# Linear attention and a folded feed-forward: the first loads on GpSimd's queue, and another order of the work

## The chip, the core and the metric

The kernel runs on one core of one Trainium2 chip. The metric is device time in microseconds for one execution, input and output in the chip's main memory (HBM). A core has five engines that run their own instruction streams and meet at semaphores: PE (TensorE, the matrix unit), DVE (VectorE), ACT (ScalarE), POOL (GpSimd) and SP (SyncE, which here only starts transfers). Transfers are started from a queue of SP, GpSimd or ACT and carried out by 16 DMA engines.

## What is computed

q, k and v are float32 of shape (8 batches, 8 heads, 576 positions, 64). Linear attention with the feature map phi(x) = elu(x) + 1 gives 4608 tokens of width 512, and a multiplicative feed-forward with two more matrices follows:

```python
q_p, k_p = (phi(q), phi(k))                       # phi(x) = where(x > 0, x, exp(x) - 1) + 1
kv = np.einsum('bhsd,bhse->bhde', k_p, v)
z = np.sum(k_p, axis=2)
num = np.einsum('bhsd,bhde->bhse', q_p, kv)
den = np.einsum('bhsd,bhd->bhs', q_p, z)[..., None] + 1e-06
x = (num / den).transpose(0, 2, 1, 3).reshape(4608, 512)
a = x @ w1          # 512 x 1024
b = x @ w2          # 512 x 1024
h = a * b @ w3      # 1024 x 1024
out = h @ w_out     # 1024 x 512
```

## The kernel before

**The fold.** Nothing nonlinear stands between w3 and w_out, so the kernel makes one matrix, wf = w3 w_out, once, and then computes out = (a * b) wf. For each of the eight blocks of 128 rows of w3, step `w` (w3_tr, L450) transposes the block on PE in eight 128x128 pieces and copies it to SBUF, and step `W` (wf_mm, L459) multiplies it with w_out in eight matmuls of 512 columns; `U` is a first half of a `W`.

**Tiles and chunks.** The 576 positions of a batch are four interleaved tiles of 128 ("J" tiles) and a remainder of 64. The remainders of two batches share a tile. The 36 tiles of 128 tokens make nine chunks of four: chunk 0 is batch 0's J tiles, chunk 1 batch 1's, chunk 2 begins with the shared remainder of batches 0 and 1 and goes on with batch 2, and so on.

**Steps.** All work is cut into small steps, and a text, ORDER, lists them by hand. Each engine executes its instructions in that order and can't pass one that waits. A name is a letter, a batch or chunk, and a part; a "+" is an alternative form of the step. The letters:

- L, M, N: load k, q, v of a batch (load_qkv, L105). Part 0 and 1 are four heads each (512 KB), 2 is all eight (1 MB), 3 is the remainder, two transfers of 64 KB.
- E, C, B: load a block of w3, half of w_out, a quarter of the columns of both w1 and w2 (two transfers). These come from GpSimd's queue[...]. I: constants (I0 the identity for transposes, on GpSimd; I2 the zeros for H). H n: n matmuls on zeros, which keep PE busy.
- x, X: exp of k, q on ACT; y, Y: minimum with 1 on DVE; z, Z: the larger of it and x + 1 on DVE. Together they are phi.
- v: v to bf16. K: k^T v and z, on PE. T: transposed q by DMA (SP's queue only). A: numerator, denominator and quotient. P, D: transposed x for the feed-forward, by PE or by DMA.
- a, b, c, d, e, f, g, r: the same for batch 0, by a way without the round trip of x through a transpose (q transposed on PE, quotient by Ln and Exp on ACT, result written straight to xt).
- F c.f: for chunk c, 128 of the 1024 columns of a and b: 8 matmuls of 512 columns, a copy on ACT and a product on DVE. h and i are F0.0 and F0.1 cut by row blocks of w1 and w2, so that they can follow batch 0's attention piece by piece.
- O c.m: 128 tokens of output, 8 matmuls; S: its store, on SP's queue. Q: the last one.

An O of any chunk needs the whole fold. An F of chunk c needs xt of its four tiles and a quarter of w1 and w2 for each two f.

**What decides when a transfer starts.** SP and GpSimd start transfers in the order of their own lists and wait in line: for a buffer (k, q, v and the w3 blocks share a pool of five 1 MB buffers, L56; the remainders have eight small ones), and, since the transfers of a queue use eight completion semaphores in turn, for the eighth transfer before. GATES (L502) adds a few waits of a load for an earlier load. In load_qkv only part 3 can go to GpSimd (with "+", L111); the big parts go to SP (L120):

```python
return nc.sync.dma_start(
    out=t[:, h0 * W:h1 * W].rearrange("p (h x) -> p h x", x=W),
    in_=src[b, h0:h1, 0:NJ * P, :].rearrange("h (p j) d -> p h (j d)", j=NJ))
```

The order of the front in before: GpSimd starts three w3 blocks and all of w_out first, while SP starts k's remainder, q and k of batch 0 by halves, then v; transposes and matmuls of the fold (w0, w1, U0, W0, ...) stand among the first steps of batch 0's attention; w1 and w2 come after, F0.0 and F0.1 last, and F0.2 to F0.7 among the first steps of batch 1's attention.

Of the kernel before, what the change touches and what calls it, by code (L numbers as in the profile page):

```python
# [18 lines left out]
def kernel(  # L19
# [11 lines left out]
    nc = tc.nc  # L31
# [73 lines left out]
    def load_qkv(name, src, b, part, alt=False):  # L105


        if part == 3:
            t = raw[name + "r", b] = ldr.tile([P, RW], F32, tag="ldr", name=f"{name}32r")
            for hh in range(2):  # L110
                (nc.gpsimd if alt else nc.sync).dma_start(  # L111
                    out=t[hh * R:(hh + 1) * R].rearrange("p (h d) -> p h d", d=D),
                    in_=src[b, hh * 4:(hh + 1) * 4, NJ * P:S, :].rearrange("h p d -> p h d"))
            return None
        if (name, b) not in raw:
            raw[name, b] = ld.tile([P, JW], F32, tag="ld", name=f"{name}32")
        t = raw[name, b]
        h0, h1 = ((0, 4), (4, 8), (0, 8))[part]
        W = NJ * D
        return nc.sync.dma_start(  # L120
            out=t[:, h0 * W:h1 * W].rearrange("p (h x) -> p h x", x=W),
            in_=src[b, h0:h1, 0:NJ * P, :].rearrange("h (p j) d -> p h (j d)", j=NJ))

# [344 lines left out]


    ORDER = """  # L470
    L0.3 E0 I0 M0.0 x0.2 N0.3 E1 X0.0 w0 y0.2 M1.3 E2 w1 L0.0 x0.0 Y0.0 M0.1 N0.0 X1.2 X0.1 C0
    w2 Z0.0 C1 U0 Z0.1 W0 L0.1 y0.0 N1.3 z0.4 N0.1 a0.0 I1 Y0.1 Z0.2 Z0.3 E3 z0.0 U1 I2 U2 v0.0+
    b0.0 x0.1 w3 v0.2 W1+ a0.1 W2 v0.1+ H9 z0.1 L1.2 E4 y0.1 b0.1 c0.0 z0.2 E5 L1.3+ U3 d0.0
    e0.0 z0.3 E6 w4+ M1.2 E7 f0.0 B0 x1.0 W3+ c0.1 w5 g0.0 U4 d0.1 y1.0 x1.2 z1.0 W4+ x1.1 e0.1
    f0.1 w6+ e0.2 v1.2+ g0.1 Y1.2 f0.2 W5 M2.3+ w7 N1.0 g0.2 B1 y1.2 y1.1 z1.1 B2 W6 z1.2 W7+
    N1.1 M0.3 e0.3 X1.0 Y1.0 h0.0 f0.3 N2.3 B3 z1.3 h0.1 M2.2 Z1.0 Z1.1 v1.0 L2.3+ z1.4 X1.1
    h0.2 g0.3 K1.0+ Y1.1 Z1.2 h0.3 Z1.4 v1.1 a1.0 L2.2 i0.0 K1.1+ b1.0 Z1.3 i0.1 F0.2 a1.1 b1.1
    X2.2 T1.1 F0.3 A1.0 F0.4 F0.5 Y2.2 X0.2 A1.1 P1.1 X2.0 P1.0+ Y2.0 F0.6 Z2.4 Z2.0 X2.1 F0.7
    P1.2 x2.0 O0.1 Y2.1 Y0.2 Z2.1 P1.3+ L3.3 Z2.2 O0.0 y2.0 Z2.3 N3.3+ z2.0 x2.2 z2.1 v2.2 N2.2
    O0.2+ x2.1 Z0.4 a2.0 b2.0+ y2.1 A1.2 z2.2 M3.2 y2.2 F1.0 L3.2 z2.4 F1.1 x3.2 v2.1 z2.3 a2.1  # L480
    v2.0 b2.1+ F1.2 F1.3 K2.0+ T0.1 K2.1+ y3.2 F1.4 X3.0 A2.0 x3.0 M4.2 F1.5 z3.4 X3.1 y3.0 r0
    z3.0 D1.1 Y3.0 F1.6 L4.3 N3.2 M4.3 O0.3 Y3.1 A2.1 F1.7 z3.1 S0.0 N4.3 S0.1 Z3.0 M3.3+ M6.3
    X3.2 S0.2 X4.2 X4.0 Z3.1 Z3.2 X4.1 Y3.2 Z3.3 O1.2 D2.0 Z3.4 O1.3+ a3.0 x4.2 O1.0+ Y4.1 y4.2
    v3.2+ N4.2 L4.2 a3.1 N6.3 v3.0+ x3.1 v3.1+ y3.1 b3.0 O1.1 b3.1 F2.0 z3.2 z3.3 T2.1 T3.1 Y4.0
    F2.1 N5.3+ z4.4 K3.0+ S0.3 Z4.0 Y4.2 F2.2 K3.1+ Z4.1 Z4.2 F2.3 Z4.3 Z4.4 A3.0 x4.0 v4.0 L5.2
    L5.3 F2.4 F2.5 A3.1 y4.0 F2.6 z4.0 z4.1 x4.1 P3.1 F2.7 A2.2 P3.2 v4.1+ P3.0 O2.2 M5.2 M5.3
    x5.0 y4.1 T4.0 P3.3+ X5.2 A3.2 x5.2 S1.2 z4.2 F3.0 X5.0 z4.3 v4.2+ y5.2 X5.1 F3.1 y5.0 F3.2
    S2.2 K4.0+ x5.1 Y5.0 K4.1+ Z5.0 y5.1 z5.0 O2.3 N5.2 Z5.1 S1.0 Y5.2 A4.0 F3.3 S1.3 v5.0+ F3.4
    A4.1 D3.1 Z5.4 D2.1 L6.3 O2.0 Y5.1 v5.2 L6.2 F3.5 Z5.2 Z5.3 F3.6 v5.1+ O2.1 X6.2 F3.7 T4.1
    S1.1 z5.1 x6.0 Y6.2 O3.3 y6.0 D4.0 z5.2 z5.3 T5.0 z5.4 O3.1+ T5.1 F4.0 A4.2 x6.2 M6.2 K5.0+  # L490
    F4.1 F4.2 K5.1+ Z6.4 X6.0 F4.3 S2.3 X6.1 A5.0 F4.4 z6.0 L7.2 Y6.0 F4.5 M7.3 N6.2 S3.1 y6.2
    L7.3 F4.6 A5.1 z6.1 Z6.0 D4.1 Z6.1 Y6.1 x6.1 N7.3 S2.1 F4.7 x7.0 x7.1 S3.3 z6.4 A5.2 S2.0
    O3.2 y6.1 O4.0+ D5.0 O4.3 X7.2 Z6.2 z6.2 S3.2 v6.2 x7.2 Z6.3 y7.1 O4.2 M7.2 S4.0 O3.0 v6.0
    F5.0 T6.0 y7.0 z6.3 v6.1 F5.1 K6.0+ Y7.2 F5.2 F5.3 K6.1+ O4.1 S3.0 X7.0 z7.0 Z7.4 X7.1 T6.1
    A6.0 y7.2 F5.4 A6.1 Y7.1 F5.5 F5.6 z7.1 F5.7 D5.1 T7.1 Y7.0 N7.2 z7.4 A6.2 S4.2 Z7.0 S4.3
    v7.1 z7.2 D6.0 Z7.1 v7.2 z7.3 O5.1 Z7.2 v7.0 O5.2+ Z7.3 D6.1 O5.0 S4.1 S5.2 F6.0 S5.1 T7.0
    F6.1 F6.2 K7.0+ K7.1+ F6.3 F6.4 A7.0 F6.5 F6.6 S5.0 A7.1 F6.7 O6.2 O5.3+ O6.0+ A7.2 O6.3+
    D7.0 F7.0 F7.1 O6.1 D7.1 F7.2 F7.3 F7.4 F7.5 F7.6 S6.0 S6.2 F7.7 F8.0 O7.3 F8.1 S5.3 F8.2
    O7.0+ S7.3 F8.3 S6.1 S6.3 O7.2 F8.4 F8.5 F8.6 F8.7 O8.3+ O8.0 O8.1 S7.0 S8.3 S8.0 O7.1 S8.1
    S7.2 S7.1 Q8.2  # L500
    """
    GATES = "E4<M0.1 L0.0<E0 L1.2<E3 M0.0<E0 M1.2<C1 N1.0<E7"  # L502
    ctx.enter_context(tc.manual_schedule())
    src = {"k": k, "q": q, "v": v}
    held = {}
    gates = dict(g.split("<") for g in GATES.split())
    OBUF = 5
# [9 lines left out]
    def step(s):  # L517
# [25 lines left out]
        elif t in "LMN":  # L543
            name = "kqv"["LMN".index(t)]
            ins = load_qkv(name, src[name], b, i, alt)
            loaded(s, ins)
        elif t == "B":
# [83 lines left out]
```

## Time and profile before

| | us |
|---|---|
| median of 8 runs | 261.21 |
| lowest, highest | 260.42, 262.31 |
| the profiled execution | 261.07 |
| its span on the core | 259.0 |

The profile is one execution. Its span runs from the core's first instruction to its last; 2.07 us of the execution lie around it. Engine times are busy times; a busy PE is one with a matmul under way. The 16 DMA engines moved 48.98 MB in the span, of which the queue of GpSimd ("software_dynamic", q0) carried 6.03 MB and that of SP ("hardware_dynamic", q1) 42.54 MB; bytes are counted as written, so a weight that is turned into bf16 counts half of what is read. 38.80 MB were read from HBM: 28.3 of q, k, v and 10.5 of weights. Median times from issue to landing:

| transfer | queue | count | size written | us to landing |
|---|---|---|---|---|
| k, whole | SP | 7 | 1024 KB | 8.4 |
| q, whole | SP | 7 | 1024 KB | 8.6 |
| q, half | SP | 2 | 512 KB | 10.3 |
| w3 block | GpSimd | 8 | 256 KB | 7.4 |
| quarter of w1 or w2 | GpSimd | 8 | 256 KB | 11.4 |
| half of w_out | GpSimd | 2 | 512 KB | 11.1 |

### The profile page before, as it was taken

The numbers are of one execution on the slowest core, as the hardware profiler recorded it, in microseconds if no ns is written. First come the engines' busy times: TensorE is split into PE (matmuls) and PEld (weight loads), VectorE is DVE, ScalarE is ACT, GpSimd is POOL, SyncE is SP. The second block draws the span as 40 slices with busy tenths as digits, with TensorE's granted clock in tenths as the row PEclk, the third lists the DMA queues.
The fourth block names the chain that finished last, engine by engine and source line by source line (L and its number), as shares of the span: only waits on it lengthen the run. The fifth ranks groups of instructions, "written<-read, shape, count | busy, mean of one in ns | idle before, by whom it ended". The sixth has DMA issues, their size and how long they took to land.

```text
span 259.0 us, 4507 instructions
## 1 busy us (share of the span) xinstructions
PE 237.0 (91%) x1656; PEld 115.8 (45%) x1673; DVE 167.9 (65%) x426; ACT 129.1 (50%) x205; POOL 21.1 (8%) x42
## 2 busy tenths in 40 slices
PE   1138999899999999999999999999999999999994
PEld 1124454445454454454444444454445444444442
DVE  0026787869988979997978589468866643424320
ACT  2048587868468664677354545736533203331321
POOL 8001655000101000000000000000000000000000
PEclk9999999999999999999999999999999999999999
DMA  6999999999898499939988985844980134003024
GB/s 96 212 261 377 303 233 237 214 344 295 294 268 271 69 343 216 316 94 258 214 178 236 375 176 122 229 117 124 224 219 27 27 64 124 0 29 133 3 82 162
DMA packets 70085, 48.98 MB, mean 189 GB/s; under 512 B 34416, under 2 KB 64368, under 8 KB 70064
## 3 DMA queue, kind: packets, MB, share of 16 engines
q1 hardware_dynamic: 63104, 42.54, 61.3%
q0 software_dynamic: 6816, 6.03, 14.1%
q8 instruction: 13, 0.21, 0.3%
q10 hardware_dynamic: 144, 0.13, 0.1%
q14 instruction: 8, 0.07, 0.1%
HBM read 38.80 MB, written 9.44 MB: 186 GB/s over the span
## 4 chain that ended last, share of the span: by engine, by line
PE 76%; DMA 17%; ACT 2%; SPq 1%; issue 1%; POOL 1%; DVE 0%; POOLq 0%
PE a_ps L371 24%; PE b_ps L371 23%; PE o_ps L390 21%; DMA w3b<-in_moe_w_dram 5%; DMA k<-in_k_dram 4%; DMA v<-in_v_dram 4%; PE kvp L199 3%; DMA xt<-xn 3%; PE nd L265 2%; SPq L111 1%; PE tp L309 1%; PE xtp L285 1%; PE o_ps L417 1%; POOL k32r L111 1%; POOL w3b L445 0%
## 5 line engine op out<-in xcount | busy, mean ns | idle before, releaser
L371 PEld LDWEIGHTS <-w_sb 128*128 128x128 bf16 x576 | 54.2, 98 | 63.6 <-issue 0.7
L377 DVE TENSOR_TENSOR ab<-a_sb,b_ps 128x512 bf16<-128x512 f32 x72 | 49.0, 684 | 47.3 <-PE b_ps L371 35.7
L371 PE MATMUL a_ps<-xt,w_sb 128*128 128x512 bf16 x288 | 75.1, 380 | 0.3 <-DMA xt<-xn 0.2
L371 PE MATMUL b_ps<-xt,w_sb 128*128 128x512 bf16 x288 | 74.9, 379 | 0.0
L376 ACT COPY a_sb<-a_ps 128x512 f32<-128x512 f32 x72 | 41.9, 585 | 57.0 <-PE a_ps L371 55.8
L390 PE MATMUL o_ps<-wf_sb,ab 128*128 128x512 bf16 x266 | 63.2, 379 | 0.7
L390 PEld LDWEIGHTS <-ab 128*128 128x128 bf16 x280 | 26.7, 98 | 30.8
L393 ACT COPY o_sb<-o_ps 128x512 f32<-128x512 f32 x24 | 14.0, 583 | 30.7 <-PE o_ps L390 30.7
L162 DVE SCALAR_TENSOR_TENSOR kj<-k,e 128x256 bf16<-128x256 f32 x64 | 23.6, 414 | 0.1
L162 DVE SCALAR_TENSOR_TENSOR qj<-q,e 128x256 bf16<-128x256 f32 x64 | 23.4, 415 | 0.1
L141 DVE TENSOR_SCALAR e<-e 128x1024 bf16<-128x1024 bf16 x32 | 13.4, 418 | 13.9 <-ACT e L137 13.9
L137 ACT ACTIVATE e<-q 128x1024 bf16<-128x1024 f32 x16 | 16.7, 1058 | 9.3 <-DMA q<-in_q_dram 9.2
L454 PE MATMUL w3p<-ident,w3b 128*128 128x128 bf16 x64 | 6.2, 254 | 15.4 <-ACT w3t L455 8.0
L137 ACT ACTIVATE e<-k 128x1024 bf16<-128x1024 f32 x16 | 16.9, 1056 | 3.8 <-DMA k<-in_k_dram 2.3
L275 DVE TENSOR_TENSOR xn<-nd,r 128x512 bf16<-128x512 f32 x28 | 18.0, 685 | 0.0
L464 PE MATMUL wf_ps<-wo_sb,w3t 128*128 128x512 bf16 x61 | 16.3, 406 | 1.3 <-ACT w3t L455 1.2
L454 PEld LDWEIGHTS <-w3b 128*128 128x128 bf16 x64 | 4.8, 114 | 17.2 <-DMA w3b<-in_moe_w_dram 9.1
L393 DVE COPY o_sb<-o_ps 128x512 f32<-128x512 f32 x11 | 7.6, 686 | 6.5 <-PE o_ps L390 6.4
L171 ACT CAST vt<-v 128x1024 bf16<-128x1024 f32 x9 | 9.3, 1047 | 2.6 <-DMA v<-in_v_dram 2.6
L464 PEld LDWEIGHTS <-w3t 128*128 128x128 bf16 x64 | 6.2, 105 | 8.1 <-ACT w3t L455 1.7
L199 PE MATMUL kvp<-vt,kj 64*128 64x130 bf16 x224 | 9.2, 217 | 0.5 <-ACT vt L171 0.5
L203 ACT COPY kvf<-kvp 128x260 f32<-128x260 f32 x14 | 5.2, 375 | 8.9 <-PE kvp L199 8.7
(81 smaller groups left out, 162.7 us busy)
## 6 DMA issues: line engine op xcount, KB each, us to landing
out_dram<-o_sb SPq DMA_DIRECT2D x31, 256.0 KB, 3.2
k<-in_k_dram SPq DMA_DIRECT2D x7, 1024.0 KB, 8.4
q<-in_q_dram SPq DMA_DIRECT2D x7, 1024.0 KB, 8.6
v<-in_v_dram SPq DMA_DIRECT2D x6, 1024.0 KB, 7.5
w3b<-in_moe_w_dram POOLq DMA_DIRECT2D x8, 256.0 KB, 7.4
v<-in_v_dram SPq DMA_DIRECT2D x4, 512.0 KB, 8.7
w_sb<-in_moe_w_dram POOLq DMA_DIRECT2D x8, 256.0 KB, 11.4
out_dram<-o_sb SPq DMA_DIRECT2D x9, 128.0 KB, 2.4
```

Of the source, the lines that this page charges most:

```text
L137: nc.scalar.activation(out=e, in_=x, func=AF.Exp)
L141: nc.vector.tensor_scalar_min(out=e, in0=e, scalar1=1.0)
L162: nc.vector.scalar_tensor_tensor(out=out, in0=x, scalar=1.0, in1=e, op0=ALU.add, op1=ALU.max)
L199: nc.tensor.matmul(kvp[:, r, i * W:(i + 1) * W], kk[rows], vv[rows], start=(n == 0), stop=(n == (NJ if r == g else NJ - 1)))
L275: nc.vector.tensor_tensor(out=dst.rearrange("p (c u) e -> p u c e", u=2), in0=v4[:, :, :, 0:D], in1=r[0:n].unsqueeze(3).to_broadcast([n, 2 ...
L371: nc.tensor.matmul(ps, w[:, kc, f * P:(f + 1) * P], xt[:, 4 * c:4 * c + 4, kc, :], start=(kc == 0), stop=(kc == KC - 1))
L376: nc.scalar.copy(out=a_sb, in_=a_ps)
L377: nc.vector.tensor_mul(out=abs_[c][:, f, :], in0=a_sb, in1=b_ps)
L390: nc.tensor.matmul(o_ps, ab[:, f, m * P:(m + 1) * P], wf_sb[:, f, :], start=(f == 0), stop=(f == FC - 1))
L393: copy_of(alt)(out=o_sb, in_=o_ps)
L454: nc.tensor.transpose(tp[:, kc, :], raw["w3", i][:, kc * P:(kc + 1) * P], ident)
L464: nc.tensor.matmul(wfs[i], w3ts[i][:, kc, :], wo_sb[:, kc, :], start=(kc == 0), stop=(kc == FC - 1))
```

## The change

Three things are changed together.

1. A big part of q, k or v can now be loaded from GpSimd's queue as well, where its step has a "+".
2. With that, all k, q, v of batches 0 and 1 (except batch 0's k remainder, which stays on SP) are loaded by GpSimd, in one line with the weights: q and k of batch 0 by halves, v of batch 0, then k1, B0, E1, C0, B1, C1, B2, E2, E3, q1, B3, E4 to E7 with v1 between. Of the later batches several loads move to GpSimd too; SP keeps 9 of its 28 big loads.
3. The order is another one throughout. At the front, batch 0's attention (a to g) stands ahead of nearly all of the fold, F0.2 to F0.7 among the fold's steps, and the fold ends (W7) among the quotients of batch 1 (A1.0, A1.1); H12 stands in place of H9, before the first step of PE. Of the transposes of q for batches 2 and 3, PE's (a, b) go and DMA's (T) come; of x's, batch 2's are now done by PE (P).

No other function is changed, and no arithmetic. The diff, with ORDER cut to its front, to the first steps of chunk 1:

```diff
@@ -117,7 +117,7 @@
         t = raw[name, b]
         h0, h1 = ((0, 4), (4, 8), (0, 8))[part]
         W = NJ * D
-        return nc.sync.dma_start(
+        return (nc.gpsimd if alt else nc.sync).dma_start(
             out=t[:, h0 * W:h1 * W].rearrange("p (h x) -> p h x", x=W),
             in_=src[b, h0:h1, 0:NJ * P, :].rearrange("h (p j) d -> p h (j d)", j=NJ))
 
@@ -468,38 +468,38 @@
     ORDER = """
-    L0.3 E0 I0 M0.0 x0.2 N0.3 E1 X0.0 w0 y0.2 M1.3 E2 w1 L0.0 x0.0 Y0.0 M0.1 N0.0 X1.2 X0.1 C0
-    w2 Z0.0 C1 U0 Z0.1 W0 L0.1 y0.0 N1.3 z0.4 N0.1 a0.0 I1 Y0.1 Z0.2 Z0.3 E3 z0.0 U1 I2 U2 v0.0+
-    b0.0 x0.1 w3 v0.2 W1+ a0.1 W2 v0.1+ H9 z0.1 L1.2 E4 y0.1 b0.1 c0.0 z0.2 E5 L1.3+ U3 d0.0
-    e0.0 z0.3 E6 w4+ M1.2 E7 f0.0 B0 x1.0 W3+ c0.1 w5 g0.0 U4 d0.1 y1.0 x1.2 z1.0 W4+ x1.1 e0.1
-    f0.1 w6+ e0.2 v1.2+ g0.1 Y1.2 f0.2 W5 M2.3+ w7 N1.0 g0.2 B1 y1.2 y1.1 z1.1 B2 W6 z1.2 W7+
-    N1.1 M0.3 e0.3 X1.0 Y1.0 h0.0 f0.3 N2.3 B3 z1.3 h0.1 M2.2 Z1.0 Z1.1 v1.0 L2.3+ z1.4 X1.1
-    h0.2 g0.3 K1.0+ Y1.1 Z1.2 h0.3 Z1.4 v1.1 a1.0 L2.2 i0.0 K1.1+ b1.0 Z1.3 i0.1 F0.2 a1.1 b1.1
-    X2.2 T1.1 F0.3 A1.0 F0.4 F0.5 Y2.2 X0.2 A1.1 P1.1 X2.0 P1.0+ Y2.0 F0.6 Z2.4 Z2.0 X2.1 F0.7
-    P1.2 x2.0 O0.1 Y2.1 Y0.2 Z2.1 P1.3+ L3.3 Z2.2 O0.0 y2.0 Z2.3 N3.3+ z2.0 x2.2 z2.1 v2.2 N2.2
-    O0.2+ x2.1 Z0.4 a2.0 b2.0+ y2.1 A1.2 z2.2 M3.2 y2.2 F1.0 L3.2 z2.4 F1.1 x3.2 v2.1 z2.3 a2.1
...
+    L0.3 M0.0+ X0.0 L0.0+ I1 Y0.0 x0.2 y0.2 M0.1+ Z0.0 x0.0 Z0.1 y0.0 I2 z0.0 z0.4 L0.1+ N0.3+
+    x0.1 H12 N0.0+ N0.1+ X0.1 L1.3+ E0 Y0.1 v0.0 L1.2+ v0.1 z0.1 y0.1 B0 v0.2+ I0 Z0.2 z0.2 Z0.3
+    E1 C0 x1.2 a0.0 B1 b0.0 C1 c0.0 M1.3+ z0.3 d0.0 e0.0 a0.1 e0.1 f0.0 f0.1 B2 E2 c0.1 y1.2 E3
+    b0.1+ M1.2+ w0 d0.1 g0.0 e0.2 e0.3 f0.2 g0.1 B3 h0.0 f0.3 E4 x1.0 g0.2 z1.4 h0.1 h0.2 g0.3
+    h0.3 i0.0 y1.0 i0.1 x1.1 w1 z1.0 F0.2 X1.2 z1.1 N1.3+ y1.1 F0.3 U0 z1.2 W0+ F0.4 E5 M2.3+
+    F0.5 Y1.2 X1.0 w2+ E6 Y1.0 Z1.0 N1.0+ w3 W1 W2+ X1.1 F0.6 U3 Z1.1 E7 N1.1+ Y1.1 w4 M2.2+
+    Z1.2 W3 v1.0+ a1.0 Z1.3 b1.0 w5 F0.7 X2.2 Y2.2 Z1.4 z1.3 w6 W4 w7 L2.2+ a1.1 v1.1+ b1.1 W5+
+    v1.2 K1.0+ L3.3+ K1.1+ L2.3+ W6 X2.0 X2.1 A1.0 Y2.0 Z2.0 x2.0 W7 N2.3+ x2.1 x2.2 A1.1 T1.1
+    P1.1 O0.0 O0.1 Y2.1 Z2.4 N2.2+ P1.0 L3.2+ y2.2 y2.0 Z2.1 M0.3+ O0.3 z2.0 y2.1 v2.1 P1.2 Z2.2
+    P1.3+ v2.0 z2.1 z2.2 X0.2 Z2.3 Y0.2 z2.4 v2.2+ A1.2 x3.0 T2.0 z2.3 O0.2 M3.3+ S0.3 F1.0 x3.2
...
     """
-    GATES = "E4<M0.1 L0.0<E0 L1.2<E3 M0.0<E0 M1.2<C1 N1.0<E7"
+    GATES = "B0<L0.1 C0<N0.1 E4<N0.1 M1.2<C1"
     ctx.enter_context(tc.manual_schedule())
```

More of the change, by code (lines that the diff above doesn't have):

```diff
@@ L477 @@
-    h0.2 g0.3 K1.0+ Y1.1 Z1.2 h0.3 Z1.4 v1.1 a1.0 L2.2 i0.0 K1.1+ b1.0 Z1.3 i0.1 F0.2 a1.1 b1.1
-    X2.2 T1.1 F0.3 A1.0 F0.4 F0.5 Y2.2 X0.2 A1.1 P1.1 X2.0 P1.0+ Y2.0 F0.6 Z2.4 Z2.0 X2.1 F0.7
-    P1.2 x2.0 O0.1 Y2.1 Y0.2 Z2.1 P1.3+ L3.3 Z2.2 O0.0 y2.0 Z2.3 N3.3+ z2.0 x2.2 z2.1 v2.2 N2.2
-    O0.2+ x2.1 Z0.4 a2.0 b2.0+ y2.1 A1.2 z2.2 M3.2 y2.2 F1.0 L3.2 z2.4 F1.1 x3.2 v2.1 z2.3 a2.1
-    v2.0 b2.1+ F1.2 F1.3 K2.0+ T0.1 K2.1+ y3.2 F1.4 X3.0 A2.0 x3.0 M4.2 F1.5 z3.4 X3.1 y3.0 r0
-    z3.0 D1.1 Y3.0 F1.6 L4.3 N3.2 M4.3 O0.3 Y3.1 A2.1 F1.7 z3.1 S0.0 N4.3 S0.1 Z3.0 M3.3+ M6.3
@@ L483 @@
[L483 to L500, printed above, removed]
+    L0.3 M0.0+ X0.0 L0.0+ I1 Y0.0 x0.2 y0.2 M0.1+ Z0.0 x0.0 Z0.1 y0.0 I2 z0.0 z0.4 L0.1+ N0.3+
@@ new lines @@
+    v1.2 K1.0+ L3.3+ K1.1+ L2.3+ W6 X2.0 X2.1 A1.0 Y2.0 Z2.0 x2.0 W7 N2.3+ x2.1 x2.2 A1.1 T1.1
+    P1.1 O0.0 O0.1 Y2.1 Z2.4 N2.2+ P1.0 L3.2+ y2.2 y2.0 Z2.1 M0.3+ O0.3 z2.0 y2.1 v2.1 P1.2 Z2.2
+    P1.3+ v2.0 z2.1 z2.2 X0.2 Z2.3 Y0.2 z2.4 v2.2+ A1.2 x3.0 T2.0 z2.3 O0.2 M3.3+ S0.3 F1.0 x3.2
+    M3.2+ F1.1 X3.0 Y3.0 K2.0+ y3.0 K2.1+ N3.3 X3.1 F1.2 S0.1 M4.3 F1.3 Z0.4 z3.0 x3.1 y3.2 N3.2
+    z3.4 X3.2 F1.4 A2.0 Y3.1 F1.5 M4.2+ T0.1 F1.6 A2.1 P2.1 L4.3 v3.2+ F1.7 Z3.0 Y3.2 D1.1 Z3.1
+    S0.0 Z3.2 O1.0 y3.1 P2.2+ X4.2 L4.2 z3.1 r0 Z3.3 v3.1 O1.1+ N4.3 v3.0+ P2.0 X4.0 z3.2 O1.3
@@ new lines @@
+    F2.0 T2.1 N5.3 z3.3 T3.0 N4.2+ Z3.4 K3.0+ X4.1 A2.2 Y4.0 Y4.2 F2.1 P2.3 K3.1+ Z4.0 x4.0 y4.0
+    F2.2 M5.3 Y4.1 O1.2 z4.0 Z4.4 A3.0 F2.3 L6.3 Z4.1 L5.3 x4.2 Z4.2 F2.4 M5.2 x4.1 P3.0+ S0.2
+    T3.1 P3.1 z4.1 Z4.3 F2.5 F2.6 A3.1 X5.0 F2.7 v4.2+ v4.0 y4.1 X5.2 L5.2 P3.2 z4.2 X5.1 S1.0
+    O2.2+ S1.1 A3.2 y4.2 P3.3+ T4.0 Y5.0 v4.1 z4.3 x5.0 O2.3+ z4.4 F3.0 F3.1 x5.1 K4.0+ K4.1+
+    y5.0 Y5.2 z5.0 Z5.4 S1.3 Z5.0 M6.3 x5.2 T4.1 F3.2 F3.3 Z5.1 D3.1 z5.1 O2.1 Y5.1 A4.0 S1.2
+    x6.2 L7.3 Z5.2 F3.4 N5.2 F3.5 S2.3 D2.1 L6.2 v5.1 y5.1 A4.1 z5.2 M6.2+ F3.6 D4.0 y6.2 F3.7
@@ new lines @@
+    X6.0 S2.2 z5.3 v5.0+ O2.0 S2.1 O3.0 Z5.3 x6.0 x6.1 O3.2 M7.3 y5.2 T5.0 L7.2 z5.4 Y6.0 O3.3
+    v5.2+ y6.0 F4.0 X6.1 X6.2 K5.0+ Y6.2 K5.1+ F4.1 Y6.1 F4.2 z6.0 F4.3 M7.2 Z6.0 N6.2 A5.0 Z6.4
+    F4.4 Z6.1 F4.5 A5.1 Z6.2 O3.1 N6.3 F4.6 T5.1 z6.4 F4.7 y6.1 v6.1 S2.0 D5.0 S3.0 v6.2 z6.1
+    z6.2 X7.0 O4.0+ Z6.3 Y7.0 x7.0 y7.0 O4.1+ S3.2 x7.2 T6.0 v6.0 O4.3 A4.2 z6.3 K6.0+ D4.1 F5.0
+    F5.1 A5.2 X7.1 K6.1+ F5.2 N7.2+ A6.0 T6.1 S3.3 Z7.0 F5.3 X7.2 F5.4 S3.1 D5.1 Y7.1 F5.5 A6.1
+    Z7.1 O4.2+ N7.3 y7.2 v7.0 S4.1 A6.2 F5.6 x7.1 F5.7 Z7.2 y7.1 Z7.3 O5.0+ z7.4 Y7.2 S4.0 D6.0
@@ L501 @@
+    S4.3 Z7.4 z7.0 S5.0 O5.1 v7.1 z7.1 O5.2+ F6.0 v7.2 z7.2 T7.1 O5.3 z7.3 K7.0+ K7.1+ F6.1 F6.2
+    F6.3 T7.0 S4.2 S5.3 A7.0 F6.4 F6.5 A7.1 F6.6 F6.7 S5.1 D7.0 O6.2+ A7.2 O6.3+ O6.0 F7.0 F7.1
+    S6.3 D7.1 S5.2 S6.0 F7.2 F7.3 F7.4 O6.1 F7.5 F7.6 F7.7 D6.1 F8.0 F8.1 S6.1 O7.1 S6.2 F8.2
+    F8.3 F8.4 F8.5 O7.3 F8.6 F8.7 S7.3 O7.0+ O8.0+ S7.1 O7.2+ S7.0 O8.1 O8.3 S7.2 S8.1 S8.0 S8.3
+    Q8.2
     """
-    GATES = "E4<M0.1 L0.0<E0 L1.2<E3 M0.0<E0 M1.2<C1 N1.0<E7"
+    GATES = "B0<L0.1 C0<N0.1 E4<N0.1 M1.2<C1"
```

## The prediction

> **What bounds the kernel now.** I read the busy table and the slices first, then busy time by stretches, then the chain of waits, then the DMA queues in two short stretches.
>
> The page's first two parts: engine, busy time and share; then tenths in 40 slices of 6.5 us.
>
> ```profile
> PE 237.0 (91%) x1656; PEld 115.8 (45%) x1673; DVE 167.9 (65%) x426; ACT 129.1 (50%) x205; POOL 21.1 (8%) x42
> ...
> PE   1138999899999999999999999999999999999994
> ```
>
> TensorE is the bound, except in the first four slices and the last. By stretches (us, then busy time and instructions of PE, PEld, DVE, ACT, POOL, then clock, DMA share, GB/s written):
>
> ```profile
> 0.00:17.00 17.00, 2.11 (x17) 1.69 (x18) 1.15 (x4) 3.75 (x5) 5.35 (x18) 1.00 0.97 167
> 17.00:26.00 9.00, 7.77 (x49) 4.23 (x50) 5.08 (x15) 6.71 (x9) 1.00 (x2) 1.00 1.11 369
> 26.00:44.00 18.00, 17.41 (x118) 9.10 (x118) 13.39 (x33) 12.49 (x18) 11.69 (x18) 1.00 1.22 257
> 44.00:63.00 19.00, 18.29 (x162) 9.52 (x161) 16.04 (x43) 14.20 (x23) 0.62 (x1) 1.00 1.22 273
> 63.00:180.00 117.00, 116.53 (x898) 56.50 (x906) 97.25 (x265) 68.19 (x112) 2.45 (x4) 1.00 0.83 219
> 180.00:255.40 75.40, 74.86 (x421) 34.79 (x424) 34.93 (x72) 23.43 (x41) 0.00 (x0) 1.00 0.35 93
> ```
>
> After 63 us PE is idle for about 1 us in 192. Nearly all lost time lies in the first 26 us, while DMA is full. A gain must come from the front. The chain of waits (start, us, what) agrees:
>
> ```profile
> 1.25 3.82 DMA w3b<-in_moe_w_dram
> ...
> 8.58 11.51 DMA k<-in_k_dram
> ...
> 27.45 9.43 DMA w3b<-in_moe_w_dram
> ...
> 38.48 10.06 DMA v<-in_v_dram
> ```
>
> The last front wait is v of batch 1, landed at 48.5. PE's timeline:
>
> ```profile
> 17.77 3.24 PE L464 MATMUL wf_ps<-wo_sb,w3t 128*128 128x512 bf16 x8
> ...
> 26.99 2.10 PE L100 MATMUL warm<-zero 128*128 128x512 bf16 x9
> ...
> 37.82 1.89 PE L464 MATMUL wf_ps<-wo_sb,w3t 128*128 128x512 bf16 x8
> ...
> 61.66 1.03 PE L371 MATMUL b_ps<-xt,w_sb 128*128 128x512 bf16 x4
> ```
>
> Eight equal matmuls take 3.24 us early and 1.89 later: with the last one's 0.38 taken off, 0.41 and 0.216 us each. The last row is the end of F0.7, 62.7 us. There before has done all of the fold, chunk 0's F units, and of batch 1 its K, A1.0, A1.1, P1.0 and P1.1. I measure the change to that same state. Last, the queues (packets, MB written, share of 16 engines), at 20 to 23 and at 35 to 38 us:
>
> ```profile
> q1 hardware_dynamic: 1244, 1.14, 109.3%
> ```
>
> ```profile
> q0 software_dynamic: 778, 0.53, 116.7%
> q1 hardware_dynamic: 97, 0.09, 11.5%
> ```
>
> SP's queue alone moves 1.14 MB in 3 us, 0.38 MB/us. GpSimd's queue, with little beside it, writes 0.53 MB of bf16, so reads up to 1.06 of float32: with the other queue 1.15 in 3 us, 0.38; if some of it was uncast remainder rows, about 0.35.
>
> [...]
>
> **The change, part by part.**
> *Loads.* No byte is added. Before, SP's and GpSimd's queues shared the DMA engines, so the first q half took 9.8 us; after, one queue brings things in the listed order. Sizes follow from the shapes (a q, k or v is 1.05 MB and 0.13 of rest; B 1.05 read, C 1.05, E 0.52). Cumulated MB: batch 0's k, q, v 3.4; B0 6.2; C0 7.7; B1 8.8; C1 9.8; B2 11.0; E3 12.1; M1.2 13.1; B3 14.15; E5 15.3; E7 17.0; N1.1 17.6. From 3 to 48.5 us the queues wrote 5.0 MB (software) and 6.8 (hardware); with the cast part doubled about 16.4 MB read, 0.36 MB/us. I take 0.37, between this and 0.38. The first w3b landed 3.8 us after issue at 1.25, of which 0.52 MB is 1.4: so landing = 3.65 + MB/0.37. Batch 0 complete 12.9, B0 20.4, B1 27.4, C1 30.1, B2 33.4, E3 36.4, M1.2 39.1, B3 41.9, E7 49.6, N1.1 51.1.
> *GpSimd's issue.* Each DMA waits for the eighth before it; 2 to 3 MB (5 to 8 us of transfer) stay in flight, so the queue shouldn't run dry. A half takes the 0.75 us of an equally fine w_sb; 1 MB I put at 1.0 to 1.5 us (no row). To N1.1 that is some 32 us of issue in 50: hidden. Buffer waits (q1 on q0's buffer, the second w3 tile on k0's) are for work done 10 us earlier. Ident stands behind B0's issue, about 13 us; only the first transposes of q need it.
> *Batch 0's attention.* k is in ACT's hands by 10, v's second half is cast at about 14. DVE has 5 minima (0.42) and 16 products (0.415) plus small ones, finishing at about 16.6; then kvz/kvn 0.8, and four Ln/Exp pairs of 1.32 in row with one w3t copy of 1.0: about 24.5; product and last h matmuls: 26.4. F0.2 can start at 26.4 and B1 lands at 27.4: the attention is hidden by one us, a thin cover; where it goes, each us late costs nearly a us.
> *H12 for H9.* H9 held PE for 2.1 us at 27, amid work. H12 lies at 9 to 14, where PE has nothing: no cost. PE idles mostly from 14 to 22 afterwards, so it may be cold again at 27[...]; I take 0.5.
> *PE from 27.6.* An F unit 1.73, W 1.73, U 0.86, w 0.45, q_tr 0.45. F0.2, F0.3 to 31.1; U0, W0 32.8; wait for B2 33.4; F0.4, F0.5 36.9; w2, w3 37.8; W1 39.5; W2 needs the w2 copy, which stands on ACT behind q1's exp (M1.2 39.1 + 1.06 + 1.0 = 41.2): to 42.9; F0.6 44.6; U3, w4, W3, q_tr, w5 47.7; F0.7 49.4; w6, W4, w7, q_tr 52.5; W5 54.2; K1.0 and K1.1 (v cast by about 52.5) 55.6; W6, A1.0, W7, A1.1, two P 60.0. Against 62.7: 2.7 us earlier.
> *Later.* Transposes of q of batches 2 and 3 leave PE (32 of 0.056, 1.8 us) and go to SP's DMA (4.8 us each, with F units to cover them); 16 xt transposes come (0.9): 0.9 us less. F, O, K, A and tail count the same. SP no longer carries the early loads, so its transposes and stores wait less.
> *Sum.* -2.7 - 0.9 + 0.5 = -3.1; I keep 0.3 back for new gaps of PE after 60 us, since before has almost none there: -2.8. The profiled execution is 261.07 (span 259.0 and 2.07 outside), so 258.3; its time is 0.14 under the median of 261.21, within their spread of 1.9.
>
> **Rivals.**
> *One queue is slower (the other side).* From 3 to 6.5 us GpSimd's queue had 95% of the engines and the two read only about 0.29 MB/us; float32 1 KB rows in 1 MB requests on it are never seen. The state above then ends 8.5 us after E7 (w7, q_tr, W5, K, W6, W7 and the small ones). Break-even is 63.6 (62.7 plus the 0.9), so E7 at 55.1, a rate of 0.33 MB/us. At 0.32 the end is 263; at 0.30, 266.5. Against it: 35 to 38 us.
> *The front's gain is given back.* DVE is busy 97 of 117 us from 63 to 180; if batch 2's phi or transposes are then late for F2, the 3 us reappear as PE gaps there: 261, no change. For it: that load. Against: batch 2's q and k land right behind N1.1, by 57, earlier than now.
> *The stream runs at 0.385 and PE stays warm.* Then only PE's own work and the w2 copy bind, the state comes at 58.6: 256.
>
> **How the numbers follow.** 0.3%, what measurement can tell here, is 0.8 us. Forecast and the faster variant 0.54 (own range 255 to 260.3), given back 0.13, slower 0.33. The range 254.8 to 263.5 takes the case of one queue down to about 0.315 MB/us and leaves out about 0.2. Faster 0.54, same 0.13, slower 0.33.
>
> **What would show it.** Right: q0 carrying the front at 0.37 MB/us of reads without gaps, v of batch 1 landed at 50 to 52, F0.2 starting at 27 to 28, PE full from there, the fold's last matmul at about 59. Wrong: GpSimd's issues much over 1.5 us, DMA share below 0.9 between 5 and 50 us, F0.0 finished after 30, or PE gaps at F1.0, F2.0.

## The result, and the profile after

| | us |
|---|---|
| before, 32 runs, median (lowest, highest) | 261.26 (260.33, 262.47) |
| changed, 11 runs, median (lowest, highest) | 258.0 (256.52, 259.93) |
| ratio, 95% interval | 0.9875 (0.9853 to 0.9897) |

The changed kernel is 3.3 us faster; the forecast was 258.3. Four executions far above the others of their kernel (263.74 us of the changed one, 262.99 and 264.32 in run 4, 266.1 in run 7) are left out of all medians and ratios, and since the first of them was the one profiled with this result, the lines below are of another execution of the changed kernel: 258.04 us, span 256.2.

The page's busy row for TensorE and its row of the slices:

```profile
PE 235.5 (92%) x1641; PEld 114.0 (45%) x1660; DVE 167.1 (65%) x425; ACT 130.5 (51%) x206; POOL 42.8 (17%) x69
...
PE   0478989999999999899999999999999999999994
```

The same stretches as before (us, then busy time and instructions of PE, PEld, DVE, ACT, POOL, then clock, DMA share, GB/s):

```profile
0.00:17.00 17.00, 5.97 (x30) 2.70 (x30) 8.16 (x24) 8.99 (x10) 14.62 (x30) 1.00 0.85 285
17.00:26.00 9.00, 7.68 (x53) 4.09 (x55) 5.39 (x13) 7.56 (x12) 4.17 (x7) 1.00 1.32 197
26.00:44.00 18.00, 16.10 (x89) 7.26 (x88) 10.11 (x22) 8.70 (x13) 7.87 (x12) 1.00 1.22 237
44.00:63.00 19.00, 18.33 (x181) 10.37 (x183) 13.51 (x38) 14.60 (x22) 11.20 (x16) 1.00 0.99 280
...
63.00:180.00 117.00, 115.26 (x894) 55.83 (x901) 97.24 (x266) 68.98 (x114) 4.97 (x6) 1.00 0.92 230
```

In the first 17 us, DVE is busy for 8.16 us where it was 1.15, and ACT for 8.99 where it was 3.75: batch 0's phi is nearly done by then. PE's busy time there is mostly H12, which computes nothing of the output. Between 63 and 180 us, PE now idles 1.74 us where it idled 0.47. PE's timeline shows the places:

```profile
27.47 1.04 PE L371 MATMUL b_ps<-xt,w_sb 128*128 128x512 bf16 x4 [0.21 <-DMA w_sb<-in_moe_w_dram]
32.51 1.04 PE L371 MATMUL a_ps<-xt,w_sb 128*128 128x512 bf16 x4 [0.76 <-DMA w_sb<-in_moe_w_dram]
...
42.57 1.04 PE L371 MATMUL b_ps<-xt,w_sb 128*128 128x512 bf16 x4 [0.26 <-DMA w_sb<-in_moe_w_dram]
...
58.68 0.40 PE L285 MATMUL xtp<-ident,xn 128*128 128x128 bf16 x4
60.99 2.10 PE L390 MATMUL o_ps<-wf_sb,ab 128*128 128x512 bf16 x9 [0.41 <-ACT wf_sb L467]
70.78 1.02 PE L371 MATMUL b_ps<-xt,w_sb 128*128 128x512 bf16 x4 [0.62 <-ACT o_sb L393]
105.31 1.02 PE L371 MATMUL b_ps<-xt,w_sb 128*128 128x512 bf16 x4 [0.69 <-DVE ab L377]
```

Waits for weights between 27 and 43 us are all under 0.8 us: PE works just behind the loads. The state that before had at 62.7 us (fold, chunk 0's F units, batch 1's A1.0, A1.1 and both P done) is reached just after the row at 58.68, at about 59.1 when the second P is counted. That is a gain of 3.6 us. The forecast put the q transposes that left PE at another 0.9 (net of the xt transposes that came), so the span should be 4.5 shorter. It is 2.8 shorter (259.0 to 256.2). The missing 1.7 us are about the three last gaps shown (0.41 + 0.62 + 0.69). The last of them is not in the profile of another execution of this kernel (run 7).

### The profile page after: what moved, and what is told of

Its sections match the earlier page's. It is cut to its first block, busy times and chain, and to the rows that moved or that the text cites. A ratio compares the mean times of both kernels' runs of the same rounds, so it can differ in the third digit from the quotient of the medians.

```text
span 262.0 us, 4477 instructions
## 1 busy us (share of the span) xinstructions
PE 236.1 (90%) x1641; PEld 114.6 (44%) x1660; DVE 166.9 (64%) x425; ACT 130.5 (50%) x206; POOL 43.1 (16%) x69
## 4 chain that ended last, share of the span: by engine, by line
PE 64%; DMA 21%; ACT 5%; DVE 5%; issue 2%; POOL 2%; POOLq 0%; DVEq 0%; ACTq 0%; SPq 0%
PE a_ps L371 20%; PE b_ps L371 19%; PE o_ps L390 18%; DMA qt<-qj 10%; DMA k<-in_k_dram 6%; DMA q<-in_q_dram 3%; DMA q32r<-in_q_dram 3%; PE nd L265 2%; PE kvp L199 2%; ACT w3t L455 2%; DVE kj L162 1%; DVE qj L162 1%; ACT e L137 1%; DVE ab L377 1%; PE xtp L285 1%
## 5 line engine op out<-in xcount | busy, mean ns | idle before, releaser
L371 PE MATMUL a_ps<-xt,w_sb 128*128 128x512 bf16 x288 | 75.9, 383 | 0.4 <-DMA w_sb<-in_moe_w_dram 0.4
L393 ACT COPY o_sb<-o_ps 128x512 f32<-128x512 f32 x22 | 12.9, 584 | 38.6 <-PE o_ps L390 38.4
L120 POOL DMA_DIRECT2D v<-in_v_dram x7 | 5.9, 847 | 72.7 <-ACT vt L171 44.1
L464 PE MATMUL wf_ps<-wo_sb,w3t 128*128 128x512 bf16 x60 | 14.6, 379 | 0.3 <-issue 0.2
L100 PE MATMUL warm<-zero 128*128 128x512 bf16 x12 | 4.1, 515 | 10.6 <-DVE zero L94 10.6
L171 ACT CAST vt<-v 128x1024 bf16<-128x1024 f32 x12 | 12.6, 1048 | 0.9 <-DMA v<-in_v_dram 0.9
L265 PE MATMUL nd<-kv,qt 64*128 64x65 bf16 x224 | 6.1, 195 | 6.6 <-DMA qt<-qj 6.6
L393 DVE COPY o_sb<-o_ps 128x512 f32<-128x512 f32 x13 | 8.9, 688 | 4.4 <-PE o_ps L390 4.4
L120 POOL DMA_DIRECT2D q<-in_q_dram x7 | 6.1, 874 | 33.4 <-ACT a_sb L376 23.6
L265 PEld LDWEIGHTS <-qt 64*128 64x128 bf16 x224 | 4.4, 97 | 12.7 <-DMA qt<-qj 7.6
```

Source lines behind the costliest of these rows:

```text
L171: copy_of(alt)(out=vt[:, :, 4 * i:4 * i + 4, 0:D], in_=raw["v", b].rearrange("p (h j d) -> p j h d", h=H, j=NJ)[:, :, 4 * i:4 * i + 4])
L265: nc.tensor.matmul(nd[0:n, u, hp * (D + 1):(hp + 1) * (D + 1)], w[rows], kvs[b][rows, hp, u, :], start=True, stop=True)
L371: nc.tensor.matmul(ps, w[:, kc, f * P:(f + 1) * P], xt[:, 4 * c:4 * c + 4, kc, :], start=(kc == 0), stop=(kc == KC - 1))
L393: copy_of(alt)(out=o_sb, in_=o_ps)
L464: nc.tensor.matmul(wfs[i], w3ts[i][:, kc, :], wo_sb[:, kc, :], start=(kc == 0), stop=(kc == FC - 1))
```

## The experiments

Runs were measured in sets, each beside the kernel before, which was at 261.0 to 261.2 us in every set; the ratios are to it. The gates (the few waits of a load for an earlier load) changed with the order and go with it in all runs but 3 and 5.

**1. The changed kernel again, and the transpose of q.** In the execution of 263.74 us PE had one gap of 5.10 us, from 76.5 us on, waiting for the DMA transpose of batch 2's q (T2.0). The first run repeats the kernel; the second one makes that transpose on PE, as before did:

```diff
-    ... x3.0 T2.0 z2.3 O0.2 M3.3+ S0.3 F1.0 x3.2
+    ... x3.0 z2.3 O0.2 a2.0 b2.0+ M3.3+ S0.3 F1.0 a2.1 b2.1 x3.2
```

> The changed kernel unchanged, for an undisturbed profile. In the profile at hand PE reaches the state that before reaches at 62.7 us (fold and chunk 0 done) at about 58.4, but then waits 5.1 us for the transposed q of batch 2, which took 15 us to land. Theory A (the front gains 4 to 4.5 us, and about 1 to 2 us of it go again at the transposes of q for batches 2 and 3): about 258 us, fold done by 57.5, a PE gap of 1 to 4 us before batch 2's quotients. Theory B (the gap belongs to that one execution; the rest of the gain is spread thinly): no gap over 0.5 us after 63 us and a front gain of only about 3.

> The changed kernel with the big transpose of batch 2's q on PE instead of DMA (16 transposes of 0.056 us, 0.9 us of PE, and two copies). Theory A (PE waits for that DMA transpose by 1 to 4 us): 1 to 2 us faster than the changed kernel, 256 to 257, no PE gap before batch 2's quotients. Theory B (no such wait in undisturbed executions): 0.9 us slower, about 259.

Measured: 258.07 (255.71 to 259.42), ratio 0.9869 (0.9787 to 0.9951), and 258.91 (257.26 to 260.77), ratio 0.991 (0.9875 to 0.9944). The repeat has no gap over 0.7 us after the front, and the kernel that doesn't need the transpose isn't faster; it is 0.8 us slower, about the 0.9 that Theory B put on the 16 transposes, though single sets differ by as much. So the 5 us gap is no part of the median. Whether the change brings such an execution now and then stays open: before makes this transpose on PE, and none of its 87 executions took over 262.94 us. In the repeat T2.0 landed at 77.46 us and PE took it up at 78.15, with little to spare.

**2. The new order without the new queue.** One line back, for the big parts; the marked remainders (L111) stay on GpSimd:

```diff
-        return (nc.gpsimd if alt else nc.sync).dma_start(
+        return nc.sync.dma_start(
```

> The changed order, but all big parts of q, k, v on SP's queue again. Theory A (what matters is that data come in the order of need, with the attention first; one line does this): SP's queue runs ahead of the weights at 0.38 MB/us, so w1 and w2's first quarter is late and shares the engines; 1 to 3 us slower than the changed kernel, 259 to 261. Theory C (the order of the work alone gives the gain, the queue is of no matter): 257.5 to 258.5. Theory D (the queue alone gives it): 261 or more.

Measured: 265.62 (264.62 to 266.34), ratio 1.0168 (1.0116 to 1.0219). Slower than before, and slower than the first two theories allowed. PE's timeline shows losses in two distant places:

```profile
20.29 0.61 PE L330 MATMUL den<-qt,kvz 128*128 128x512 bf16 x1 [2.31 <-DVE kvz L320]
...
82.42 1.86 PE L371 MATMUL a_ps<-xt,w_sb 128*128 128x512 bf16 x4 [4.98 <-ACT a_sb L376]
```

Batch 0's attention is late (after the wait of 2.31 us its matmuls also ran slow, or cold: 0.61 us each for 0.38, and the granted clock from 17 to 26 us was 0.64), and at 77 us PE stands for 5 us. W6, at 54.53 in the changed kernel, begins at 56.83.

**3. The new queue with the old order.** Before's ORDER and gates, with the changed line of load_qkv and a "+" on all loads of batches 0 and 1 except batch 0's k remainder (of its gates only those of E4 and M1.2 are kept). The later batches' big loads stay on SP:

```diff
-    L0.3 E0 I0 M0.0 x0.2 N0.3 E1 X0.0 w0 y0.2 M1.3 E2 w1 L0.0 ...
+    L0.3 E0 I0 M0.0+ x0.2 N0.3+ E1 X0.0 w0 y0.2 M1.3+ E2 w1 L0.0+ ...
```

> Before's order, with q, k, v of batches 0 and 1 on GpSimd's queue in the order of the text (two gates kept, the four that tie a load to a w3 block dropped). Theory A: the order of the old text asks for w3 and w_out ahead of k and v, so batch 0's attention stays late; 260.5 to 263. Theory C (order alone): 261 to 262. Theory D (queue alone): 258 to 259.

Measured: 268.17 (268.13 to 268.7), ratio 1.0273 (1.0227 to 1.0318). Slower than any of the theories allowed. PE waits for w_out, now in line behind q and k, and later for the copy of the second half of batch 1's v, which landed late:

```profile
18.64 1.87 PE L464 MATMUL wf_ps<-wo_sb,w3t 128*128 128x512 bf16 x4 [5.97 <-DMA wo_sb<-in_moe_w_out_dram]
...
55.81 0.70 PE L199 MATMUL kvp<-vt,kj 64*128 64x130 bf16 x9 [5.65 <-ACT vt L171]
```

So the order alone loses, and so does the queue where it carries batches 0 and 1 only. The next three runs ask which loads matter.

**4. The two groups of loads apart.** With the new order, either the first two batches (`alt and b >= 2` decides for GpSimd) or only the later ones (`alt and b < 2`) go back to SP. The same condition goes into the line of the remainders (L111):

```diff
-        return (nc.gpsimd if alt else nc.sync).dma_start(
+        return (nc.gpsimd if alt and b >= 2 else nc.sync).dma_start(
```

> The changed order, batches 0 and 1 back on SyncE's queue, the later batches' marked loads stay on GpSimd's. The run with everything marked back on SyncE lost 7.5 us: about 2.3 us of it was there at W6 (56.8 for 54.5), 5 us was one PE gap at 77-82 us where q of batch 3 stood in SyncE's line behind a transpose. Theory A (the two are separate): 260-261, PE late by about 2 us at W6, no PE gap over 1 us at 70-85. Theory B (the later gap follows from the late front): the gap at 77-82 stays, 264-266.

> The changed order, batches 0 and 1 on GpSimd's queue as in the changed kernel, the marked loads of batches 2 and later back on SyncE's. Theory A (front and later part separate): W6 at 54-55, then a PE gap of 4-5 us where q of batch 3 is issued behind the transpose and stores on SyncE; 262-263.5. Theory B (the gain sits in the first two batches alone, as the change's title says): 257.5-258.5, no gap over 1 us. Theory C (batch 2's loads on SyncE overtake batch 1's on GpSimd, as in the run with the old order): v or q of batch 1 lands over 10 us after issue, and PE waits for it before 57 us; 260 or more.

| new order: batches 0, 1 from | later marked loads from | us | ratio, interval |
|---|---|---|---|
| GpSimd | GpSimd (the change) | 258.0 | 0.9875 (0.9853 to 0.9897) |
| SP | GpSimd | 260.1 | 0.9967 (0.9933 to 1.0001) |
| GpSimd | SP | 266.31 | 1.019 (1.0154 to 1.0227) |
| SP | SP (run 2: remainders on GpSimd) | 265.62 | 1.0168 (1.0116 to 1.0219) |

With the other group on GpSimd, the front's queue is worth 2.4 us by the ratios, the later loads' queue 8.2. The two don't add up: with the later loads on SP, moving the front's loads gains nothing (266.31 and 265.62).

With batches 0 and 1 on SP there is no gap at 77 us, as Theory A said, but the front is late: the first o_ps matmul of chunk 0 starts at 62.87 for 59.13. The loads were not in one line any more. Batch 1's two v halves were issued at 35.1 and 36.3 from SP, beside weights and batch 2's q from GpSimd; that is 8 us earlier than in the changed kernel (43.07 and 44.60), and yet they landed about 4 us later. Their landing times, and those of the same two in the changed kernel:

```profile
DMA to landing us min/median/max: 18.2/18.3/18.3
```

```profile
DMA to landing us min/median/max: 5.4/5.9/6.4
```

With only the later loads on SP, the front is as good as the change's (first o_ps at 58.60), and then PE stands for 7.06 us:

```profile
81.68 1.86 PE L371 MATMUL a_ps<-xt,w_sb 128*128 128x512 bf16 x4 [7.06 <-ACT a_sb L376]
```

Theory A in kind, though it put the gap at 4 to 5 us. SP's issues ahead of it:

```profile
56.62 0.45 SPq L120 DMA_DIRECT2D k<-in_k_dram  x1
66.90 1.32 SPq L242 DMA_TRANSPOSE qt<-qj  x1
68.27 1.34 SPq L111 DMA_DIRECT2D q32r<-in_q_dram  x2
...
70.48 0.37 SPq L120 DMA_DIRECT2D q<-in_q_dram  x1
```

and the data rate of that kernel's DMA from 62 to 72 us, in 40 slices:

```profile
GB/s 385 381 389 389 393 287 66 78 0 0 0 0 0 0 0 0 0 0 0 0 0 0 0 0 127 289 292 290 291 291 287 276 164 44 116 264 371 349 262 86
```

SP issued no transfer between 57 and 66.9 us: the transpose T2.0 waits for batch 2's phi of q, and the loads stand behind it. The DMA engines run dry for 4 us (16 slices of 0.25 us with nothing). q of batch 3, the last row, was issued at 63.27 in the changed kernel, where GpSimd's line has no transpose in it; here it lands at 78.6, ACT waits 8.6 us for it (its exp stands ahead of the a_sb copies), and PE waits for those copies. In run 2 the same wait ends at 82.42, 0.7 us later than here, though its front was 2.8 us later (first o_ps at 61.43): what an earlier front gains is mostly waited away. Part of that may be the remainders, which stand in SP's line only here (the row at 68.27).

This wait cost more than itself: the matmuls after it ran at about half the rate (four in 1.86 us for 1.03). From 81.68 us, twelve F matmuls with sixteen small ones among them took 5.69 us; in the changed kernel the same mix takes 3.05 (76.33 to 79.38).

**5. The old order with batch 2's loads in the same line.** As run 3, and M2.2, L2.2, N2.2 and N2.3 get a "+" as well:

```diff
-    N1.1+ M0.3+ e0.3 ... N2.3 B3 z1.3 h0.1 M2.2 Z1.0 ... L2.2 i0.0 ... N2.2
+    N1.1+ M0.3+ e0.3 ... N2.3+ B3 z1.3 h0.1 M2.2+ Z1.0 ... L2.2+ i0.0 ... N2.2+
```

> As the run with the old order and the first two batches on GpSimd's queue (268.2), with batch 2's loads put on that queue too, behind v of batch 1. Theory A (SyncE's loads of batch 2 overtook v's second half, which landed 14 us after issue): the wait of 5.65 us at 55.8 us shrinks under 1.5 us, v's second half lands within 5 us, and the time falls to 263-265; what is left is the early waits for w_out and w3. Theory B (v was late because it was issued late, behind GpSimd's gated weights): the wait at 55.8 stays over 4 us, 267-269.

Measured: 261.09 (259.94 to 262.68), ratio 1.0001 (0.9983 to 1.0019). Theory A in kind, though more came back than it said: the wait at 55.8 is gone, and 7.1 us with it. That is about the 5.65 us and the 1.7 more that run 3 lost to slow matmuls after the wait (4.13 us from 55.81 for what takes 2.41 here). v was issued at 40.65 us in run 3 and at 39.63 here, so a late issue (Theory B) isn't the cause. From 40 to 55 us, queues and landings of run 3 (packets, MB, share; then transfers with their us to landing):

```profile
q0 software_dynamic: 3030, 2.26, 82.3%
q1 hardware_dynamic: 1724, 1.73, 41.4%
...
v<-in_v_dram POOLq DMA_DIRECT2D x1, 512.0 KB, 14.0
w_sb<-in_moe_w_dram POOLq DMA_DIRECT2D x2, 256.0 KB, 13.4
```

and of this run:

```profile
q0 software_dynamic: 3558, 3.73, 117.1%
...
v<-in_v_dram POOLq DMA_DIRECT2D x1, 512.0 KB, 8.3
w_sb<-in_moe_w_dram POOLq DMA_DIRECT2D x2, 256.0 KB, 5.6
```

In run 3, SP's queue moved 1.73 MB of batch 2's loads, which are used only later, while v of batch 1 and the weights, needed at once, took 14.0 and 13.4 us. In one line they took 8.3 (Theory A said within 5) and 5.6. What was asked for earlier on one queue had no precedence here over the other's: in run 3 batch 2's k (1 MB, SP) was issued at 41.21 us, 0.56 after that half of v (0.5 MB, GpSimd), and landed at 52.3, v at 54.7. The old order with one line is still only as fast as before: PE waits 3.86, 0.82, 5.56 and 0.73 us for weights in the first 21 us, since q and k now stand ahead of w_out.

**6. The warm-up.** Only H12 is taken out; nothing of the output depends on it:

```diff
-    x0.1 H12 N0.0+ N0.1+ X0.1
+    x0.1 N0.0+ N0.1+ X0.1
```

> The changed kernel without H12, the twelve warming matmuls on zeros; what is computed stays. Theory 'the warm-up is free and spares nothing' (the forecast held that the PE is cold at 27 us either way, and cost 0.5 us): 257.5-258.5, batch 0's attention as long as before. Theory 'the twelve matmuls at 9.9-14.5 us carry TensorE's clock into batch 0's attention': the den and num matmuls take about 0.63 us instead of 0.38 as they do in the run with the order on SyncE, the stretch from the first transpose (14.4) to the last h matmul (25.9) grows by 1-2 us, the granted clock of 17-26 us is under 0.8, and the time is 259-260.

Measured: 256.89 (256.16 to 257.74), ratio 0.9834 (0.9786 to 0.9882). Both theories had a part. PE does run cold without it:

```profile
17.66 0.61 PE L330 MATMUL den<-qt,kvz 128*128 128x512 bf16 x1 [0.73 <-DVE kvz L320]
...
20.82 0.40 PE L219 MATMUL kvp<-vt,kj 128*128 128x130 bf16 x4
...
27.56 1.03 PE L371 MATMUL a_ps<-xt,w_sb 128*128 128x512 bf16 x4
```

The den matmul takes 0.61 us where H12 made it 0.39; PE is warm from about 20.7 us (four kvp matmuls in 0.40 us, where they took 0.64 at 15.30). (The clock column of the stretches doesn't show it: 1.00 from 17 to 26 us. The lengths of the matmuls do.) F0.2 starts at 27.56 instead of 26.23. But the waits for w_sb at 27, 32 and 34 us, together 1.29 us in the changed kernel, are then gone, and W7 starts at 55.45, within the 54.98 to 56.49 of five profiles with H12. So H12 warms PE as meant, but no gain from it is seen: the loads set the pace. That the time is even lower without it is within what single sets differ by (next run).

**7. The small gaps after the front.** The copy of wf's last block (W7) stood on ACT behind an exponential that waits for batch 2's k; the third o_sb copy stood behind one that waits for q32r. Both are moved; a second kernel leaves H12 out too; the third is the changed kernel itself, in the same set:

```diff
-    Y2.0 Z2.0 x2.0 W7 N2.3+ x2.1 ... z2.3 O0.2 M3.3+
+    Y2.0 Z2.0 W7 x2.0 N2.3+ x2.1 ... z2.3 O0.2+ M3.3+
```

> The changed kernel with two evictions moved: the last wf_sb copy (W7) ahead of batch 2's first k exponential (x2.0) on ScalarE, and the third o_sb copy of the first chunk (O0.2) on VectorE in place of ScalarE. Theory A (the part of the front's gain that is missing at the end went into these small PE gaps: 0.4-1.0 us at the second o_ps behind the exponential that waits for k, 0.5-0.6 us at F1.0 behind an exponential that waits for q32r): both gaps under 0.2 us, 0.8-1.2 us less than the changed kernel of the same call, about 257.0. Theory B (PE has slack there, the gaps come back at the next eviction or transfer): gaps gone but new ones of the same sum by 110 us, time within 0.4 us of the changed kernel's.

> The same two evictions moved, and no H12 either. The run without H12 alone was at 256.9 with PE cold (0.63 us a matmul) until 20 us, and its F phase began no later, since the weights' landing sets it. Theory A (the warm-up is worth nothing either way): as the run with the two evictions alone, within 0.5 us. Theory B (leaving it out is a gain of its own): 0.7-1.2 us less than that run, about 256.

> The changed kernel unedited, run beside the two versions with the evictions moved, so that differences under one per cent can be read within one call: 257.7-258.4; the profile shows the gaps of 0.4 us or more at the second o_ps (behind the wf_sb copy) and at F1.0 (behind the o_sb copy).

| | us | ratio, interval |
|---|---|---|
| two evictions moved | 257.54 | 0.9862 (0.9821 to 0.9904) |
| and no H12 | 256.6 | 0.9812 (0.9773 to 0.9851) |
| changed kernel | 256.86 | 0.9816 (0.978 to 0.9853) |

In its profile the kernel with the evictions moved has lost the gap at the second o_ps (1.05 us in the changed kernel's profile of this set), but at F1.0 one of 0.82 stands, now behind an a_sb copy: the exponential that waits for q32r stands ahead of that one too. In the profile of the version without H12 neither gap is left (that execution took 254.82), but its median is no better either. Their times are not below that of the changed kernel. Theory A, 0.8 to 1.2 us less than the changed kernel beside it, falls; none of these versions is shown to beat the change. The changed kernel was at 258.0, 258.07 and 256.86 in three sets (the last below the 257.7 to 258.4 expected), so a difference of 1 us between sets says nothing.

## Why the prediction was right

The time was right (258.3 for 258.0), and so was the front's mechanism in the main: one line of loads in the order of need, with PE working just behind it. The closeness of the number is luck in part. One wait in the front was wrongly derived, terms of the sum were mis-sized in opposite directions, and a large effect that the sum didn't contain was created by one half of the change and removed by the other.

- *Landing = 3.65 + MB/0.37.* Right. Said and measured: B1 27.4, 27.47; M1.2 39.1, 39.88; B3 41.9, 42.57; N1.1 51.1, 51.0 (issued at 44.60, 6.4 to land). The measured ones of B1, M1.2 and B3 are the starts of the instructions that wait for them.
- *GpSimd's issue.* A half took 0.75 us as said, 1 MB 0.90 where I put 1.0 to 1.5. Hidden either way.
- *Batch 0's attention.* Said to end at 26.4; F0.2 starts at 26.23, one us ahead of B1. The thin cover held. DVE's last product of batch 0's phi ended at 17.2 (said: 16.6).
- *H12 costs nothing, PE may be cold at 27 (0.5 us, my own estimate).* The first half is right. The second isn't: PE didn't idle mostly after H12 but was busy for 7.68 of the 9 us from 17 to 26, its longest idle time was 1.67 us, and it stayed warm (0.38 to 0.39 us for each den, num and F0 matmul; in run 2 den and num took 0.61 to 0.63 after 2.31 us of idle time). Where H12 was left out (run 6), PE was cold until 20.7 us, and the load waits took that up whole.
- *W2 gated by the w2 copy behind q1's exp, W2 to 42.9, F0.6 to 44.6.* Wrong. The step is "w2+", and its "+" sends the copy to VectorE; the copy on ACT behind q1's exp is w3's. W1 and W2 (16 matmuls) ran without a break and ended at 41.0; then F0.6 waited for its load (B3), and its matmuls were through at about 43.4. PE's two rows, DVE's copy for w2 and ACT's for w3:

```profile
37.36 3.62 PE L464 MATMUL wf_ps<-wo_sb,w3t 128*128 128x512 bf16 x16
41.27 1.04 PE L371 MATMUL a_ps<-xt,w_sb 128*128 128x512 bf16 x4 [0.29 <-DMA w_sb<-in_moe_w_dram]
```

```profile
37.48 0.68 DVE L455 COPY w3t<-w3p 128x1024 bf16<-128x1024 bf16 x1
```

```profile
40.84 0.99 ACT L455 COPY w3t<-w3p 128x1024 bf16<-128x1024 bf16 x1
```

- *The state reached 2.7 us earlier.* It was 3.6: 59.1 for the 60.0 of the forecast's chain, to which the 0.5 for cold PE came on top. PE was 0.4 us ahead of the chain at the end of F0.5 and 1.2 at the end of F0.6; the wait for the w2 copy that wasn't there makes most of it.
- *0.3 us kept for new gaps of PE after 60 us.* It was about 1.7. With the 0.9 for the q transposes, the sum by the profile is -3.6 - 0.9 + 1.7 = -2.8, the same as -2.7 - 0.9 + 0.5 + 0.3. A front 1.4 us better than forecast and gaps 1.4 us worse cancel, which is luck. That the gaps really cost 1.7 isn't shown: two of them were attacked in run 7, where one went and no time came back.
- *Transposes of q on SP's queue, 4.8 us each.* T2.0 took 9.4 us in the profile shown, where F units covered it by less than a us (run 1); in the execution of 263.74 us it took 15.0, and the median of the six was 7.0.
- *"SP no longer carries the early loads, so its transposes and stores wait less."* This was costed at nothing, and the moved loads of later batches weren't costed at all. The run with only those back on SP (266.31) shows what hangs on them: 8.3 us. The new order makes T2.0 a DMA transpose at 67 to 68 us; were the loads still in SP's line, they would stand behind it. A part of the diff that looks like a companion of the main part was the larger one.
- *Rivals.* One slower queue: no, the landings above follow 0.37 MB/us; from 4 to 12 us the queue wrote 2.89 MB, 0.36 MB/us, where break-even was put at 0.33. The gain given back at batch 2's phi or transposes: in one profile only (run 1), at the transpose. The stream at 0.385 and PE warm: PE was warm (0.38 to 0.39 us a matmul), and the state came close to the 58.6 named there, but its 256 left no room for the gaps that came later.

## What to carry to other kernels

Where two queues feed one stream of work, don't count on the time at which a transfer was asked for to rank it: in run 3 batch 2's k, asked for 0.56 us after v of batch 1 on the other queue, landed 2.3 us before it. Put what is needed in one order into one line, with the next stage's loads behind it (v then took 8.3 us for 14.0, run 5). The other way round, keep loads off a queue that also carries instructions which wait for computed data: with the later loads behind T2.0 in SP's line the DMA engines ran dry for 4 us, and the kernel took 266.31 us for 258.0 (run 4). And of a change with two halves, run each half alone, but expect that neither may gain: here the order alone cost 4.4 us, the queue for the first two batches alone 7 (nothing, with batch 2's loads in the line too), and both together gained 3. Last, before a step is put on an engine in a forecast, read its mark in the order: the copy of "w2+" was on another engine than assumed.

## What wasn't expected of the hardware

GpSimd's queue moved float32 in larger packets than SP's queue. In the changed kernel, from 3 to 13 us:

```profile
q0 software_dynamic: 1003, 3.43, 95.0%
```

3.43 MB in 1003 packets, 3.4 KB each, where SP's queue before had 1.14 MB in 1244 (20 to 23 us), 0.9 KB each. The rate was no higher for it: 0.34 MB/us in these 10 us, which have the start in them, 0.36 from 4 to 12, against 0.38. And one DMA transpose of a batch's q took 15.0 us to land in the execution of 263.74 us, where the median of the four in the kernel before is 4.8; what held it up there is open.
